# A long convolution and a state-space scan on one core: stages cut into quarters and halves of TensorE's array, rows laid out by parity, five chunks transposed on TensorE, and a new order of work

## The chip, the core and the metric

The kernel runs on one core of a Trainium2 chip. The metric is the device time of one execution in microseconds (us), lower is better; a comparison is made from several executions of both kernels on the same chip. The core has five engines with a queue each: TensorE (PE in the profile, its weight loads PEld), VectorE (DVE), ScalarE (ACT), GpSimd (POOL) and SyncE (SP). Each works off its own list of instructions in order and waits for the others through semaphores. SP and POOL issue the transfers. Matmul results go to PSUM, which is used here as eight banks of 128 rows x 512 float32; ACT and DVE copy them from there to on-chip memory as bfloat16.

## What is computed

Two independent layers on sequences of 2048 rows x 1024 channels; their results stand side by side in the output.

```python
# A: a causal convolution with a filter as long as the sequence
k_shift = sum(k_pad[:, t:t+S, :] * shift_k[:, 3-t] for t in range(4))   # 4 taps
kv = k_shift * v
y  = irfft(rfft(kv, 2S) * rfft(ssm_k, 2S))[:S]
a  = q * (y + kv * ssm_D)
# B: a diagonal complex recurrence over the rows
Bu = x @ B_bar.T
h[t] = Lam_bar * h[t-1] + Bu[t]
b  = 2 * Re(h @ Cmat.T) + x * Dskip
out = concat([a, b], axis=-1)
```

Inputs and output are bfloat16.

## The kernel before

**Layer A** is a transform of 4096 points in two stages. Row s of the sequence is 16 m + (n2), with m = 0..127 and n2 = 0..15, and a tile holds for one or two n2 the 128 rows m, one on each partition. `kvm`, `kva`, `kvb`, `kvc` (DVE) make kv for one n2 from a ring of k tiles (`kp` loads two of them, `vp` two of v). Neighbouring m belong to two interleaved half-length sequences of parity p = m % 2, so the first stage `am` has to transform the even and the odd m apart: for one n2 and one half of the channels it issues two matmuls of the whole 128 x 128 array, with a constant F1 whose rows of the other parity are zero. `ae` copies the two banks out, `ast` stores them to a DRAM buffer, from which they come back in another layout (`lk`). The filter goes the same way: `hl` loads, `hT` transposes on PE, `hc` copies, `hm` transforms, `he` and `hst` store, `lh` reloads. `hm` is already cut into quarters: four matmuls of 64 x 64, two row halves by two column halves, which stand next to each other and write two banks. The second stage (`sk`, `sh`, with a constant from one of three W slots that `lw` loads), a swap of partitions by DMA (`sw`, `swp`), the product (`pr`, DVE) and the inverse second stage (`sa`) follow, all in 64 x 64 quarters. `sae` copies, `vst` stores to a third DRAM buffer Vs, `vl` reloads by n2, and the last stage `a3` brings both parities back into 128 rows, by two full-array matmuls that add up in one bank, again with a half-zero constant G. `a3e` copies it out, `qm` (DVE) multiplies by q (`qp`), and `ost` (POOL) or `osp` (SP) stores two n2 at a time.

**Layer B** takes 16 chunks i of 128 rows. `x.i` loads a chunk transposed, by a transposing DMA on SP. `U.i.jp.jl` is 16 matmuls of 128 x 128 with weights BT; four such pairs make a chunk. `ue` copies them out, `r1` and `r2` (DVE) rotate, `cy` carries the last column over, `sc` (DVE) scans, `r3` and `r4` rotate back, and `y` (full-array matmuls, 5 chunks) or `yq` (64 x 64 quarters, 11 chunks) forms the output with weights CT; `ye`, then `yst`, `ysp`, `ysg`, `ysh` store. At the start `bl`/`bT`/`bc` load, transpose and copy the weights BT, and `cl`/`cT`/`cc` or `cx` (transposing DMA) do it for CT.

**The order** is written out by hand: one string of 1,489 words, each a call such as `U.0.2.0:a34p4` with the places it takes (a: on-chip memory, p: PSUM bank, w, h: W slot and scan slot). The words run in that order, so each engine's list is the string with the other engines' words left out. Which engine copies a bank out is in the word too: `sae` is ACT, `saev` DVE.

A word waits for its inputs and for its places to be free. Bank places bind PE to the engine that empties them, and the in-order lists bind what stands behind a waiting word. The lines of the profile: L417 transposes (bT, cT), L433 and L441 their copies, L468 U, L473 ue, L515 and L518 y, L533 yq, L602 am, L608 ae, L626 hT, L631 hc, L651 hm, L682 sh and sk, L708 pr, L720 sa, L731 vst, L736 vl, L741 qp, L748 a3, L755 a3e, L449 x, L666 lw.

Of the kernel before, what the change touches and what calls it, by code (L numbers as in the profile page):

```python
# [16 lines left out]
BF16 = mybir.dt.bfloat16  # L17
# [15 lines left out]
def a_constants():  # L33
# [31 lines left out]
    return f(F1), f(FQ), f(G), f(W)  # L65
# [3 lines left out]
bl.7.0:a32 wbe.2 bl.0.1:a34 exp1 wb.4:p3 dve2 bl.5.0:a33 dve3 bT.2.0:p6 wb.6:p2 wbe.5 bl.4.0:a49 sm_pre wbe.4  # L69
bl.4.1:a17 exp2 wb.3:p7 bl.1.1:a47 bc.2.0 wb.7:p6 wbe.3 sin0 kp.1 bT.0.1:p0 bT.7.0:p4 wbe.7 wbe.6 bl.6.1:a16 bT.4.0:p1  # L70
bc.0.1 bc.7.0 bl.0.0:a46 tabA1:a24a51a14a12 kp.-1 bT.1.1:p2 x.0:a47 par_rest cl.0.0:a39 wb.1:p7 bT.5.0:p5 sin1
bl.3.0:a31 bcv.4.0 bT.0.0:p3 wbe.1 bT.4.1:p6 bc.1.1 tabA2 kring bl.3.1:a46 kvm.3:a26 gz bT.6.1:p1 bc.0.0 bl.1.0:a23
bc.4.1 U.0.2.0:a34p4 U.0.0.0:p2 sin2 bc.6.1 bl.2.1:a22 bT.3.1:p0 bc.5.0 x.1:a33 eo kvm.2:a18 kvm.1:a40 U.0.2.1
bT.1.0:p5 kva.2 cT.0.0:p1 bT.2.1:p3 bc.2.1 bT.3.0:p6 kva.1 kvb.2:a38 kva.3 bc.3.0 U.1.2.0:a36p7 stt U.1.2.1 bl.6.0:a50
bT.6.0:p3 kvb.1:a46 bl.7.1:a32 bc.3.1 U.0.1.0:p6 bT.7.1:p0 kp.-2 bc.1.0 bc.6.0 bc.7.1 U.0.1.1 U.0.0.1 ue.0.0 ue.0.1
vp.1:a48 cl.2.0:a22 z2 z1 cl.1.1:a31 cc.0.0 x.3:a21 cl.2.1:a44 ue.1.2 ue.0.2 U.0.3.0:p3 U.0.3.1 kvb.3:a32 ue.0.3
U.1.3.0:p6 U.1.0.0:p2 kvm.0:a13 cT.2.0:p0 U.1.3.1 U.1.1.0:p5 kvc.3 kvc.2 kva.0 r1.0:a48 cc.2.0 lw.1:w0 cl.1.0:a30
ue.1.3 cx.5.1 U.1.0.1 ue.1.0 cT.1.0:p3 cc.1.0 cl.3.0:a45 kvb.0:a39 am.2.1:p4p0 ae.2.1.1:a28 rta r2.0:h0 am.2.0:p6p2
cT.2.1:p1 cc.2.1 U.1.1.1 ue.1.1 cT.3.0:p3 vp.0:a42 kvc.1 U.3.2.0:a34p7 cc.3.0 ae.2.0.1 kvc.0 ae.2.0.0 kp.3 sc.0.1
U.3.2.1 hl.0.1:a24 cl.3.1:a20 cT.3.1:p0 sc.0.0 cc.3.1 am.3.0:p5p1 ae.3.1.0:a22 ae.2.1.0 r1.1:a42 hl.0.0 U.3.3.0:p3  # L80
U.3.3.1 cT.1.1:p0 cc.1.1 kp.2 hl.1.0:a48 cl.0.1:a38 ue.3.2 am.3.1:p4p1 ae.3.1.1 U.3.0.0:p6 ue.3.3 U.3.0.1 ue.3.0
ae.3.0.0 hl.1.1 am.1.1:p0p2 ae.1.1.1:a30 cx.5.0 am.0.0:p1p7 ae.0.1.0:a18 ae.3.0.1 r3.0:a12 hdv.1 ast.2 hdv.0 ast.3
U.3.1.0:p3 r4.0 ae.0.0.0 U.3.1.1 x.2:a52 cT.0.1:p5 am.1.0:p6p4 hT.0.4:p7 r2.1:h1 ae.1.0.1 am.0.1:p0p1 hT.0.7:p2
ae.1.1.0 hc.0.4:a16 hT.0.3:p4 ae.1.0.0 hT.0.0:p7 kvm.6:a12 ue.3.1 hT.0.6:p6 hc.0.3:a17 ae.0.0.1 cy.1 cc.0.1 ld_Q
hc.0.0:a46 ae.0.1.1 U.2.1.0:a44p3 r1.3:a40 U.2.1.1 ast.1 sc.1.1 U.2.2.0:p4 hc.0.7:a23 U.2.2.1 U.2.0.0:p5 ast.0 lw.0:w1
cx.6.0 cx.6.1 ue.2.2 U.2.0.1 cx.4.1 ue.2.1 hc.0.6:a20 ue.2.0 r2.3:h2 hT.0.1:p3 hT.0.2:p7 hc.0.1:a22 sc.1.0
hm.0.6.1:p1p2 hm.0.6.0:p4p6 he.0.6.0.0:a34 U.2.3.0:p0 hT.0.5:p3 hc.0.2:a41 U.2.3.1 hm.0.3.0:p5p4 he.0.6.1.1 he.0.6.1.0
# [24 lines left out]
he.1.0.0.0 he.1.0.0.1 he.1.0.1.1 yq.3.6 hm.1.1.0:p1p2 he.1.1.0.0 yq.3.7 ye.3.0:a26 kva.10 ysp.2 hm.1.6.0:p6p3 ast.8
# [78 lines left out]
def full_kernel(ctx, tc, A_q, A_k, A_v, A_shift_k, A_ssm_k, A_ssm_D, B_x, B_Lre, B_Lim, B_Bre, B_Bim,  # L191
# [645 lines left out]
```

## Time and profile before

| | |
|---|---|
| runs shown, us | 351.59 median of 3 (350.28, 351.59, 355.09) |
| profiled execution, first to last instruction, us | 346.5 (the page gives no other time for it) |
| granted TensorE clock | 0.998 of full speed |
| busy us: PE, PEld, DVE, ACT, POOL | 328.0, 237.5, 325.2, 272.3, 69.3 |
| DMA | 101.09 MB, mean 292 GB/s |
| U matmuls (L468) | 2048, 122.6 us busy |
| yq matmuls (L533, 64 x 512) | 1408, 87.6 us busy |
| am matmuls (L602, 128 x 512) | 54 recorded of 64, 16.4 us busy |
| a3 matmuls (L748, 128 x 512) | 61 recorded of 64, 15.1 us busy |
| transposing loads of x (L449) | 16, median 6.2 us to landing |

How to read it: matmuls overlap, so their busy times sum to more than the clock shows, and four quarters of one set run at once; what a matmul costs is read from the starts in the timeline, not from its duration. Some matmul records are missing, so a count of "x12" can stand for 16. A wait that is listed for an engine is idle time of that engine just before the instruction named, put down to what ended it. "PEclk" was at full speed throughout, so times of PE need no correction.

### The profile page before, as it was taken

The numbers are of one execution on the slowest core, as the hardware profiler recorded it, in microseconds if no ns is written. First come the engines' busy times: TensorE is split into PE (matmuls) and PEld (weight loads), VectorE is DVE, ScalarE is ACT, GpSimd is POOL, SyncE is SP. The second block draws the span as 40 slices with busy tenths as digits, with TensorE's granted clock in tenths as the row PEclk, the third lists the DMA queues.
The fourth block names the chain that finished last, engine by engine and source line by source line (L and its number), as shares of the span: only waits on it lengthen the run. The fifth ranks groups of instructions, "written<-read, shape, count | busy, mean of one in ns | idle before, by whom it ended". The sixth has DMA issues, their size and how long they took to land.

```text
span 346.5 us, 11774 instructions
## 1 busy us (share of the span) xinstructions
PE 328.0 (95%) x5086; PEld 237.5 (69%) x5105; DVE 325.2 (94%) x263; ACT 272.3 (79%) x520; POOL 69.3 (20%) x114
## 2 busy tenths in 40 slices
PE   5889899999999999999999999999699999999994
PEld 2678789654856777688957877775376789754442
DVE  3999799999999999999999999999799999999991
ACT  6999999998999884599668899899689893314741
POOL 5000002142343163121100222211021133000021
PEclk9999999999999999999999999999999999999999
DMA  6999999979979879997896689999998898998995
GB/s 214 340 292 261 354 271 275 254 264 307 334 248 248 281 245 301 281 241 277 303 343 205 226 313 344 262 353 330 276 289 297 312 334 287 295 391 270 340 405 205
DMA packets 62752, 101.09 MB, mean 292 GB/s; under 512 B 29422, under 2 KB 31742, under 8 KB 62700
## 3 DMA queue, kind: packets, MB, share of 16 engines
q1 hardware_dynamic: 52652, 65.81, 63.7%
q0 software_dynamic: 10048, 34.52, 27.8%
q8 instruction: 40, 0.66, 0.8%
q14 instruction: 12, 0.10, 0.1%
HBM read 52.08 MB, written 33.55 MB: 247 GB/s over the span
## 4 chain that ended last, share of the span: by engine, by line
PE 68%; ACT 17%; DVE 7%; DMA 4%; issue 2%; SPq 1%; DVEq 0%; ACTq 0%
PE bank L468 24%; PE bank L533 15%; PE bank L515 10%; PE bank L682 4%; PE bank L720 4%; ACT BT L433 4%; PE bank L748 3%; PE bank L602 3%; DVE gslot L499 3%; PE bank L651 2%; ACT arena L608 2%; DMA wslot<-a_c_W 2%; ACT CT L441 2%; DVE arena L486 2%; ACT arena L473 2%
## 5 line engine op out<-in xcount | busy, mean ns | idle before, releaser
L468 PEld LDWEIGHTS <-BT 128*128 128x128 bf16 x2048 | 116.2, 98 | 13.0 <-issue 8.2
L468 PE MATMUL bank<-arena,BT 128*128 128x128 bf16 x2048 | 122.6, 219 | 1.6 <-DMA arena<-in_B_x_dram 0.9
L533 PE MATMUL bank<-CT,gslot 64*64 64x512 bf16 x1408 | 87.6, 377 | 0.0
L499 DVE TENSOR_TENSOR_SCAN gslot<-rtab,gslot 128x1040 bf16<-128x1040 f32 x32 | 73.0, 2312 | 0.1
L533 PEld LDWEIGHTS <-gslot 64*64 64x64 bf16 x1408 | 43.4, 107 | 23.9 <-ACT arena L698 0.6
L473 ACT CAST arena<-bank 128x512 bf16<-128x512 f32 x63 | 38.8, 655 | 11.6 <-PE bank L468 11.6
L608 ACT CAST arena<-bank 128x512 bf16<-128x512 f32 x64 | 37.2, 670 | 5.8 <-PE bank L602 4.9
L515 PE MATMUL bank<-CT,gslot 128*128 128x512 bf16 x154 | 38.1, 380 | 0.6 <-issue 0.3
L691 ACT CAST arena<-bank 128x512 bf16<-128x512 f32 x59 | 32.5, 615 | 7.8 <-PE bank L682 7.2
L486 DVE TENSOR_TENSOR arena<-arena,Z 128x4096 bf16<-128x4096 bf16 x16 | 36.5, 2284 | 2.2 <-ACT arena L473 2.1
L708 DVE TENSOR_TENSOR arena<-arena 128x4096 bf16<-128x4096 bf16 x16 | 36.3, 2285 | 1.7 <-ACT gslot L495 0.8
L728 ACT CAST arena<-bank 128x512 bf16<-128x512 f32 x61 | 33.3, 630 | 5.4 <-PE bank L720 5.3
L486 DVE TENSOR_TENSOR arena<-gslot,Z 128x4096 bf16<-128x4096 bf16 x16 | 36.6, 2288 | 0.3
L698 ACT CAST arena<-bank 128x512 bf16<-128x512 f32 x61 | 34.2, 616 | 3.3 <-PE bank L682 2.8
L659 ACT CAST arena<-bank 128x512 bf16<-128x512 f32 x64 | 35.2, 689 | 1.0 <-PE bank L651 0.7
L551 ACT CAST arena<-bank 128x512 bf16<-128x512 f32 x29 | 17.7, 616 | 16.3 <-PE bank L533 8.7
L582 DVE TENSOR_TENSOR arena<-arena 128x4096 bf16<-128x4096 bf16 (+3 forms) x16 | 30.0, 1886 | 0.1
L662 POOL DMA_DIRECT2D Ys_h<-arena x32 | 22.9, 728 | 29.0 <-ACT arena L659 23.1
L611 POOL DMA_DIRECT2D Ys_kv<-arena x16 | 10.9, 688 | 87.1 <-ACT arena L608 71.8
L515 PEld LDWEIGHTS <-gslot 128*128 128x128 bf16 x160 | 14.0, 98 | 17.1 <-issue 2.6
L702 POOL DMA_DIRECT2D arena<-arena x20 | 10.7, 538 | 70.8 <-ACT arena L691 46.9
L682 PE MATMUL bank<-arena,wslot 64*64 64x512 bf16 x256 | 21.5, 381 | 3.0 <-DMA wslot<-a_c_W 3.0
(104 smaller groups left out, 427.7 us busy)
## 6 DMA issues: line engine op xcount, KB each, us to landing
Ys_kv<-arena POOLq DMA_DIRECT2D x16, 512.0 KB, 4.9
Ys_h<-arena POOLq DMA_DIRECT2D x32, 256.0 KB, 3.8
arena<-Ys_h SPq DMA_DIRECT2D x16, 512.0 KB, 5.3
arena<-Ys_kv SPq DMA_DIRECT2D x16, 512.0 KB, 6.4
Vs<-arena POOLq DMA_DIRECT2D x16, 512.0 KB, 5.8
arena<-Vs SPq DMA_DIRECT2D x16, 512.0 KB, 6.9
arena<-arena POOLq DMA_DIRECT2D x20, 256.0 KB, 4.1
arena<-in_A_k_dram SPq DMA_DIRECT2D x8, 512.0 KB, 6.0
```

Source lines behind the costliest of these rows:

```text
L468: nc.tensor.matmul(pu[:, w, jl, :], BT[:, 2 * jp + jl, w, d, :], xT[:, d, :], start=(d == 0), stop=(d == ND - 1))
L473: either("ue", lambda cp, i, jp: cp(st["u", i][:, :, 2 * jp:2 * jp + 2, :], st.pop(("pu", i, jp))))
L486: nc.vector.tensor_mul(m, s_, win(Z))
L499: nc.vector.tensor_tensor_scan(gf, rtab[:].rearrange("p j t -> p (j t)"), gf, 0.0, ALU.mult, ALU.add)
L515: nc.tensor.matmul(py, h[:, w, j, 2:GW], CT[:, j, w, dh * 512:(dh + 1) * 512], start=(j == 0 and w == 0), stop=False)
L533: mm = nc.tensor.matmul(st["py", i, dh][cols, cs(r)], lhs(dh, rows, c), rhs(dh, rows), start=first, stop=last)
L608: cp(st["ysb", n2][:, p, dh * 512:(dh + 1) * 512], st.pop(("pa", n2, p, dh)))
L659: cp(o, st.pop(("pb", hf, s, e, r)).rearrange("p (n c t) -> p n c t", n=2, c=2))
L682: nc.tensor.matmul(st["ps", nm, g, l][64 * dh:64 * dh + 64, :], st["w", i][rows, a * WC:a * WC + 64], st[nm, i][rows, a, dh * 512:(dh + 1) ...
L698: cp(st["x16", i][:, a, l, :], st.pop(("ps", "k", g, l)))
L708: nc.vector.tensor_mul(hab, st.pop(("x16", i)).rearrange("p a l d -> p (a l d)").unsqueeze(1).to_broadcast([P, 2, 2 * D]), hab)
L728: cp(st["vsb", i][:, a, dh * 512:(dh + 1) * 512], st.pop(("pv", g, dh)))
```

## The change

*Rows by parity.* k, v, q tiles and the A half of the output now hold row m = 2 n + p on partition 64 p + n, so that each parity fills one half of the partitions. The loads of earlier k rows (`kp` with r < 0) need three transfers in place of two.

*First stage in quarters.* `am` issues four 64 x 64 matmuls with FQ, the constant that `hm` already uses; F1 and its load are gone.

*Last stage in column halves.* `a3` issues two matmuls of 128 rows x 64 columns with a small G, one for each parity, into the two halves of one bank.

*Five x chunks* (11 to 15) are loaded plainly (`xn`), transposed by eight matmuls on PE (`xt`) and copied to their place by ACT (`xc`) or DVE (`xcv`).

*Stores.* `ost` and `osp` store one n2 (256 KB) instead of two: 16 stores, not 8.

*Order.* The string is new, 1,506 words. Beside the words above: DVE's evictions a3ev 7 to 1, saev 3 to 0, yev 3 to 0, shev 5 to 3, uev 1 to 2, bcv 1 to 0 (the other engine ACT takes or gives them), hd 2 to 4 and hdv 2 to 0, sw 20 to 23 and swp 12 to 9.

```diff
-    F1 = np.stack([tr * (m % 2 == p)[:, None] for p in range(2)], axis=1)
     FQ = np.concatenate([tr[::2], tr[::2]], axis=0)
-    G = np.stack([tr.T * (m % 2 == p)[None, :] * 2 / NFFT for p in range(2)], axis=1)
+    G = tr.T[:, ::2] * 2 / NFFT
...
 ORDER = """
-bl.5.1:a45 bT.5.1:p6 ld_par par_T:p1 bc.5.1 bl.2.0:a25 ld_F ld_w:a26 wb.0:p0 kp.0:a0 p32 wb.2:p4 wbe.0:a8 dd wb.5:p5
+ld_par par_T:p1 p32 exp1 dd ld_w:a30 wb.2:p4 wb.3:p0 wb.6:p5 wbe.2:a8 bl.3.0:a46 wb.0:p3 bl.6.1:a18 dve2 wbe.3 wb.5:p6
...
-    kr, vr, qr, oar = (a.rearrange("(m s) d -> m s d", s=16) for a in (k, v, q, out_a))
+    kr = k.rearrange("(m s) d -> m s d", s=16)
+    kpr, vr, qr, oar = (a.rearrange("(n p s) d -> p n s d", p=2, s=16) for a in (k, v, q, out_a))
...
+    def xn(i):
+        st["xn", i] = sb(1)
+        spd(st["xn", i], x[i * T:(i + 1) * T, :])
+    E["xn"] = xn
+    E["xt"] = lambda i: tr_(("xn", i), ("xp", i))
...
+    def xc(cp, i):
+        st["xT", i] = sb(1).rearrange("p (d t) -> p d t", d=ND)
+        cp(st["xT", i], st.pop(("xp", i)))
+    either("xc", xc)
...
         if r >= 0:
-            spd(t_, kr[:, 2 * r:2 * r + 2, :])
+            spd(t_, kpr[:, :, 2 * r:2 * r + 2, :])
         else:
-            spd(t_[1:113, :, :], kr[0:112, 16 + 2 * r:18 + 2 * r, :])
-            spd(t_[113:P, :, :], kr[112:P - 1, 16 + 2 * r:18 + 2 * r, :])
+            spd(t_[64:P, :, :], kr[0:P:2, 16 + 2 * r:18 + 2 * r, :])
+            spd(t_[1:49, :, :], kr[1:97:2, 16 + 2 * r:18 + 2 * r, :])
+            spd(t_[49:64, :, :], kr[97:127:2, 16 + 2 * r:18 + 2 * r, :])
...
     def am(n2, dh):
         for p in range(2):
             st["pa", n2, p, dh] = bank()
-            nc.tensor.matmul(st["pa", n2, p, dh], F1t[:, p, :], st["kv", n2][:, dh * 512:(dh + 1) * 512], start=True, stop=True)
+        for a in range(2):
+            for p in range(2):
+                rows, cols = slice(64 * p, 64 * p + 64), slice(64 * a, 64 * a + 64)
+                nc.tensor.matmul(st["pa", n2, p, dh][cols, :], FQt[rows, cols],
+                                 st["kv", n2][rows, dh * 512:(dh + 1) * 512], start=True, stop=True)
...
         for p in range(2):
-            nc.tensor.matmul(pt, Gt[:, p, :], st["vv", n2][:, p, dh * 512:(dh + 1) * 512], start=(p == 0), stop=(p == 1))
+            nc.tensor.matmul(pt[64 * p:64 * p + 64, :], Gt[:], st["vv", n2][:, p, dh * 512:(dh + 1) * 512], start=True, stop=True)
...
-    E["ost"] = lambda r: gpd(oar[:, 2 * r:2 * r + 2, :], st["ot", r])
-    E["osp"] = lambda r: spd(oar[:, 2 * r:2 * r + 2, :], st["ot", r])
+    E["ost"] = lambda n2: gpd(oar[:, :, n2, :], st["ot", n2 // 2][:, n2 % 2, :])
+    E["osp"] = lambda n2: spd(oar[:, :, n2, :], st["ot", n2 // 2][:, n2 % 2, :])
```

What the new order does is seen in the engines' lists. On ACT, near the end of the start phase, before the first copy of a transposed filter tile (COPY to arena, 128x1024, L631 before), the list ran:

```order
L608 CAST arena<-bank_98 128x512
L608 CAST arena<-bank_103 128x512
L608 CAST arena<-bank_100 128x512
L608 CAST arena<-bank_97 128x512
L608 CAST arena<-bank_96 128x512
L608 CAST arena<-bank_100 128x512
L631 COPY arena<-bank_103 128x1024
L608 CAST arena<-bank_102 128x512
```

The same stretch of ACT's list now (L618 is the copy of am, L467 of U, L438 of CT, L641 of hT):

```order
L618 CAST arena<-bank_100 128x512
L618 CAST arena<-bank_96 128x512
L618 CAST arena<-bank_99 128x512
L618 CAST arena<-bank_97 128x512
L467 CAST arena<-bank_101 128x2x256
L467 CAST arena<-bank_102 128x2x256
L438 COPY CT<-bank_98 128x8x128
L641 COPY arena<-bank_96 128x1024
```

Ahead of that copy stand three more copies of am and one more of BT than before, and behind it those that moved.

On PE, am.4.0 stood among the full-array matmuls of y.1.1 (bank_99 the output of y, F1t the masked constant):

```order
L518 MATMUL bank_99<-Dd,arena 128x128
L602 LDWEIGHTS F1t
L602 MATMUL bank_103<-arena,F1t 128x512
L602 LDWEIGHTS F1t
L602 MATMUL bank_102<-arena,F1t 128x512
L515 LDWEIGHTS gslot_90
```

Now it stands between two parts of the same y as four quarters (FQt; L611 is am, L520 and L523 y; the two matmuls are issued a second time for the other column half):

```order
L523 MATMUL bank_101<-Dd,arena 128x128
L611 LDWEIGHTS FQt
L611 MATMUL bank_96<-arena,FQt 64x512
L611 LDWEIGHTS FQt
L611 MATMUL bank_100<-arena,FQt 64x512
```

The rows behind these are the same two banks once more and then y's next matmul on L520: the array goes from 128 x 128 to 64 x 64 and back around one am. In the string before, PE's words change between full-array work and quarters 64 times; in the new one they change between full-array work, quarters and column halves 196 times, 28 of them to or from the halves.

In the tail of PE's list, an a3 before (Gt the constant of the last stage, bank_98 its output, between y.14 and y.15):

```order
L518 MATMUL bank_102<-Dd,arena 128x128
L748 LDWEIGHTS Gt
L748 MATMUL bank_98<-arena,Gt 128x512
L748 LDWEIGHTS Gt
L748 MATMUL bank_98<-arena,Gt 128x512
L515 LDWEIGHTS gslot_90
```

And the last a3 now, between two parts of y.15:

```order
L523 MATMUL bank_97<-Dd,arena 128x128
L758 LDWEIGHTS Gt
L758 MATMUL bank_101<-arena,Gt 64x512
L758 LDWEIGHTS Gt
L758 MATMUL bank_101<-arena,Gt 64x512
L520 LDWEIGHTS gslot_90
```

Both matmuls of the word now have 64 output rows and go to the two halves of one bank.

More of the change, by code (lines that the diff above doesn't have):

```diff
@@ L71 @@
[L71 to L75, printed above, removed]
@@ new lines @@
+cy.9:h1 sh.12:p2p3 she.12.0:a44 yq.8.0:p6p7 she.12.1 U.10.0.1 she.13.0 r2.9 sk.12:p3p4 yq.8.1 she.13.1 sa.11:p0p2
+lk.7:a1 ske.12.0:a42 sa.10:p5p3 ue.10.0 ske.12.1 sae.11.0:a12 lk.8:a51 yq.8.2 lw.8:w2 pr.4 yq.8.3 sae.10.1 sk.13:p4p0
+sae.11.1 sc.9.1 sae.10.0 ske.13.0 xt.11:p2 sa.9:p5p3 yq.8.4 xc.11:a14 sa.8:p2p4 yq.8.5 sae.9.1:a29 sae.9.0 sc.9.0
+ske.13.1 sh.17:p5p1 sae.8.1 she.17.0:a35 sh.16:p3p0 yq.8.6 vst.2 ysp.7 she.16.1 she.16.0 sk.17:p4p5 sw.6.0 yq.8.7
+she.17.1 sae.8.0 ye.8.1:a34 ske.17.0:a9 U.11.3.1:p3 sw.6.1 U.11.3.0 sk.16:p7p2 ske.17.1 ske.16.1 pr.6 sa.13:p5p0
@@ L488, in full_kernel, with g_ @@
     E["r1"] = lambda i: rot_mul(i, st.pop(("u", i)), Z1)
+    def g_(i):
+        if ("g", i) not in st:
+            st["g", i] = gslots[cur["h"].pop(0)]
+        return st["g", i]
     def r2(i):
[L491 removed]
         m = mview(i)
[L493 removed]
+        nc.vector.tensor_add(g_(i)[:, :, :, 2:GW], m[:, :, 0, :, :], m[:, :, 1, :, :])
     E["r2"] = r2
[L495 removed]
+    E["cy"] = lambda i: nc.scalar.copy(g_(i)[:, :, :, 1], st["g", i - 1][:, ::-1, :, GW - 1])
     def sc(i, a):
```

270 lines of the change are left out of this document (129 added, 141 removed).

## The prediction

> **What bounds the kernel now.** I read the page first (busy time, chain), then the busy time by stage, then what PE itself waited for, then the timelines at the places that the change touches.
>
> ```profile
> span 346.5 us, 11774 instructions
> PE 328.0 (95%) x5086; PEld 237.5 (69%) x5105; DVE 325.2 (94%) x263; ACT 272.3 (79%) x520; POOL 69.3 (20%) x114
> PE 68%; ACT 17%; DVE 7%; DMA 4%; issue 2%; SPq 1%; DVEq 0%; ACTq 0%
> ```
>
> PE and DVE are both nearly full, and the chain goes mostly through PE. The stages tell them apart (columns: PE, PEld, DVE, ACT, POOL busy us with counts, clock, DMA share, GB/s):
>
> ```profile
> 45.00:60.00 15.00, 14.89 (x234) 13.83 (x234) 15.00 (x12) 15.00 (x28) 2.86 (x5) 1.00 1.11 270
> 60.00:75.00 15.00, 14.67 (x156) 8.73 (x155) 15.00 (x13) 15.00 (x29) 4.74 (x7) 1.00 0.99 263
> 285.00:300.00 15.00, 15.00 (x271) 13.53 (x272) 14.64 (x9) 6.72 (x14) 3.38 (x5) 1.00 0.83 287
> ```
>
> Up to about 60 us ACT has no free moment: it copies every BT, CT and U out of PSUM, and PE's eight banks come free at ACT's pace. Later ACT has room (6.72 of 15). DVE is full in the middle too, but hardly anyone on PE waits for it. PE's waits:
>
> ```profile
> PE bank L417 <- DMA arena<-in_B_B_im_dram: 4.7, 2, 3.5
> PE bank L682 <- DMA wslot<-a_c_W: 3.0, 1, 3.0
> PE bank L468 <- DMA arena<-in_B_x_dram: 0.9, 1, 0.9
> PE bank L720 <- DVE arena L708: 0.7, 1, 0.7
> ```
>
> The first and third lie in the first 18 us. Behind 60 us PE has two waits worth a line, 3.0 for a W slot and 0.7 for DVE's product. So the model is: ACT sets the pace to about 55 us, and from there the time is PE's matmuls laid end to end, plus a few us.
>
> **The change part by part.** *Cheaper matmuls.* The masked pairs of am and a3 are 2 x 32 words of two 128x512 matmuls each:
>
> ```profile
> 28.72 5.52 PE L468 MATMUL bank<-arena,BT 128*128 128x128 bf16 x96
> 34.08 0.61 PE L417 MATMUL bank<-ident,arena 128*128 128x128 bf16 x8
> 302.72 0.20 PE L533 MATMUL bank<-Dd,arena 64*64 64x64 bf16 x4
> 303.61 0.20 PE L533 MATMUL bank<-Dd,arena 64*64 64x64 bf16 x4
> 320.01 2.75 PE L748 MATMUL bank<-arena,Gt 128*128 128x512 bf16 x12
> 322.60 1.03 PE L515 MATMUL bank<-CT,gslot 128*128 128x512 bf16 x4
> ```
>
> Starts tell the rate: twelve 128x512 matmuls take 322.60 - 320.01 = 2.59, so 0.216 each and 0.43 a word; a 128x128 one takes 5.36 / 96 = 0.056; four quartets of 64x64 quarters and one small quartet take 303.61 - 302.72 = 0.89, so a quartet takes at most 0.22 (I use 0.216). am's 32 words go from 0.43 to 0.216: -6.9 us, certain as to its rate, since FQ quarters run so today (L651). a3's two column halves, 64 outputs from 128 rows, stand in no row. Run side by side they take 0.216 a word (-6.9), one after the other 0.43 (0). I take the former, by the quarters, the nearest row in which column halves share one bank.
>
> *Changes of array shape.* This is what the change adds. Counting along PE's order from start to end, the step from full-array matmuls to quarters or halves, back, or between these two comes 64 times before and 196 times now. Its price:
>
> ```profile
> 64.43 1.06 PE L468 MATMUL bank<-arena,BT 128*128 128x128 bf16 x16
> 65.42 0.41 PE L651 MATMUL bank<-arena,FQt 64*64 64x512 bf16 x4
> 65.76 1.04 PE L515 MATMUL bank<-CT,gslot 128*128 128x512 bf16 x3
> 66.64 0.22 PE L518 MATMUL bank<-Dd,arena 128*128 128x128 bf16 x1
> 66.79 0.41 PE L651 MATMUL bank<-arena,FQt 64*64 64x512 bf16 x4
> ```
>
> Sixteen matmuls from 64.43 end at 65.32, the quartet starts at 65.42: 0.10 lost. It is through at 65.64, and the next starts at 65.76: 0.12. At 66.64 the gap is 0.15 in place of 0.056: 0.09. So 0.10 a step, 0.2 for in and out. A lone quartet between full-array work then costs 0.42, as much as the masked pair that it replaces; only am words that lie beside other quarters gain (20 of the runs of quarters now are am alone, 22 words). In all (196 - 64) x 0.10 = +13.2, the 28 steps to and from the halves at the same price (these no row shows: 0 to 0.12 each, so up to 2.8 less). The Trainium skill, "TensorEngine Tiling (Array Packing)", section Tiling Modes, says that changing the mode drains TensorE, with no time; it would make the halves pay too.
>
> *x through TensorE.* Five chunks take 8 transposes each and a copy.
>
> ```profile
> 40.23 0.61 PE L417 MATMUL bank<-ident,arena 128*128 128x128 bf16 x8
> 40.68 1.06 PE L468 MATMUL bank<-arena,BT 128*128 128x128 bf16 x16
> L449 SPq DMA_TRANSPOSE arena<-in_B_x_dram x16: 1237/1575/4278, 13.2 to 275.4; - x16
> arena<-in_B_B_re_dram SPq DMA_DIRECT2D x8, 256.0 KB, 4.7
> ```
>
> Eight take 0.45, so 5 x 0.45 = +2.2 on PE. The Trainium skill, "TensorE: Matmul & The Clock Gate", Part 4, gives about 275 ns for one transpose in a kernel; by that the term would be 11.0 and the end 8.8 later, but the row has 0.056 from start to start, and I keep it. The copies, of the size of a BT copy (0.90 on ACT, below), go four to ACT and one to DVE, under PE's work. SP's issue of a chunk falls from 1.6 (median; the row has min/median/max) to the 0.34 of a plain one (last row of the tail below), 5 x 1.2 = 6 us late and off PE's path. But xt now makes PE itself wait for the plain load. Four have 7.7 us or more of PE work between xn and xt; xt.13 has 3.4 (r4.9 frees its place just before), and a 256 KB load lands after 4.7 (the row of B's loads, median). Behind xt.13 on PE stand sa.17, yq.9.2 and all that follows, though U.13 needs the chunk some 41 us later. So 0.34 + 4.7 - 3.4 = 1.6 at most, nothing if DVE is ahead there; I take +0.8.
>
> *ACT at the start.* The first hT copy (L631) is a place that both orders pass. Before it ACT now has 16 BT copies instead of 15 (bcv.4.0 was DVE's) and 16 am evictions instead of 13; CT, U and the rest are equal.
>
> ```profile
> 25.35 5.61 ACT L433 ACTIVATE BT<-bank 128x1024 bf16<-128x1024 bf16 x6
> 30.77 1.15 ACT L473 CAST arena<-bank 128x512 bf16<-128x512 f32 x2
> 48.59 0.78 ACT L608 CAST arena<-bank 128x512 bf16<-128x512 f32 x1
> 49.07 1.28 ACT L473 CAST arena<-bank 128x512 bf16<-128x512 f32 x2
> 53.45 1.21 ACT L631 COPY arena<-bank 128x1024 bf16<-128x1024 bf16 x1
> ```
>
> A BT copy takes 0.90, an eviction 0.48: 0.9 + 3 x 0.48 = +2.3, and 0.3, my choice without a row, because ACT's first copy now waits for the parameters: the place moves from 53.45 to about 56.1, +2.6. ACT is the pace there, so cheaper am words gain nothing ahead of it. PE is also less far: 22 U words (16 matmuls, 0.89 each) are behind it, not 24, so 2 x 0.89 = 1.8 is still to come, and 8 am words, not 7.
>
> *DVE.* Evictions that DVE gives up (6 a3e, 3 sae, 3 ye, 2 she) against those it takes (one ue, one x copy), and bcv away: 13 fewer.
>
> ```profile
> L755 DVE CAST arena<-bank 128x512 bf16<-128x512 f32 x7 | 4.8, 681 | 0.0
> ```
>
> About 13 x 0.68 = 8.8 us, and two adds of 0.2 go to ACT. By the waits above this is worth at most the 0.7 on L720; I take 0.9 off, with the small gap beside it.
>
> *Rows by parity, stores, tail.* Loads of k, v, q keep their bytes and run lengths; two kp words issue one DMA more. out's A half leaves in 16 stores of 256 KB, not 8 of 512; POOL and SP issue them between other things. The way through Vs must still be hidden:
>
> ```profile
> 286.65 1.06 PE L720 MATMUL bank<-arena,wslot 64*64 64x512 bf16 x16
> 290.17 0.72 POOL L731 DMA_DIRECT2D Vs<-arena  x1 [1.90 <-ACT arena L728]
> 294.77 3.90 SPq L736 DMA_DIRECT2D arena<-Vs  x6
> 305.75 1.47 PE L748 MATMUL bank<-arena,Gt 128*128 128x512 bf16 x5
> DMA to landing us min/median/max: 4.5/6.9/7.9
> 341.89 0.22 PE L518 MATMUL bank<-Dd,arena 128*128 128x128 bf16 x1
> 342.76 0.34 SPq L555 DMA_DIRECT2D out_dram<-arena  x1
> ```
>
> From the last sa (ends 287.6) PE had 18.1 us of other work before the first a3. The chain under it is 2.5 to the last store, 4.6 to the first load, three issues of 0.65 and 6.9 (the landing row is that of the loads from Vs): 16.0. Now PE has 17.3 there (11 U words, 7 yq.12 words of 0.89, one x, some steps). It just holds. From the last matmul (341.89) to the end there are 4.6 us of eviction and store; that stays.
>
> *The sum*, on the span of 346.5: ACT's start +2.6; U left over +1.8; am behind that place 25 x 0.43 to 24 x 0.216 = -5.6; a3 -6.9; x +2.2 and +0.8; steps behind that place 182 instead of 64, +11.8; DVE -0.9; the 3.0 wait for a W slot, whose reload has 4.1 to 4.7 us of PE work now against 4.1 to 4.9, taken as half gone, -1.5. That is +4.3, so a span of 350.8. The shown runs have a median of 351.59 (350.28 to 355.09), 5.1 above the profiled span; so 355.9, which I call 356, or +1.2%. Two per cent, about what a measurement of this kernel can tell from no change, is 344.6 and 358.6.
>
> **The rivals.**
>
> *Cheap steps* (14%). If a step costs half where PE would wait anyway, 5.9 comes off: 350. If all new ones were free, 11.8: 344, faster. Against: PE hardly waits behind 60 us, so there is little to hide in, and where it waits that wait is itself time.
>
> *DVE was the bound* (10%, faster). DVE is busy 15.00 of 15 in two of the windows above. If PE only kept step with it, 8.8 fewer us on DVE give 346.5 - 8.8 + 5.1 = 343. Against: PE's 0.7 us of waiting for DVE.
>
> *Halves in a row* (12%, slower). If the second half of an a3 waits for the first, its 6.9 is not gained: 363, +3%. It decides once a word takes more than 0.30 (358.6 - 355.9 = 2.7, over 32 words 0.08 above 0.216). For: both halves use the same 128 rows.
>
> ```profile
> L748 PEld LDWEIGHTS <-Gt 128*128 128x128 bf16 x64 | 5.8, 98 | 6.7 <-issue 0.5
> ```
>
> Against: these 98 ns loads use the same rows as the matmul ahead, and matmuls still follow at 0.216. The Trainium skill, "TensorE: Matmul & The Clock Gate", Part 3, has weight loads overlap matmuls only where the row group differs, which would put the halves in a row; this trace's full-array stream contradicts it.
>
> *A new wait* (14%, slower at its upper end). The Vs chain has 1.3 us in hand; a last store that lands at 7.9 or a late sae uses that up, a W slot can again cost 3.0, and xt.13 twice what I took: 358 to 361.
>
> **How the numbers follow.** Forecast 50%: 356, by itself 351 to 360, a tenth of it over 358.6. Slower: halves 12, new wait 11, forecast's upper end 5: 28%. Faster: DVE 9, free steps 3: 12%. Within 2%: 60%. The range runs to halves in a row, 363, and down past cheap steps with both new waits gone (350 - 0.8 - 1.5) to 346, where the halves' steps are free too (28 x 0.05 at half price, 1.4); the faster cases are the tenth left out below.
>
> **What would show it.** In the profile after: steps between shapes with gaps of 0.09 to 0.12, about 196 of them; the first hT copy near 56 us; a3 words 0.216 apart; PE still the chain's main engine with no more than 3 to 5 us of waits behind 60 us; DVE near 316 busy with idle time that costs nothing. I am wrong if the steps cost nothing, if the first hT copy comes before 53 us, or if PE waits for DMA in the tail.

## The result: 65% slower, and the profile after

The kernel after takes 577.95 us (573.9 to 579.25), the kernel before on the same chip 350.93 (median of four); the ratio is 1.65, with a 95% interval of 1.64 to 1.67. Some executions of a kernel run some per cent slower than its others; the ratios leave these out, and so do the times of the experiments below. The forecast of 356 and all its rivals are far off. The profiled execution has a span of 577.4 us.

First the page of the kernel after (busy time, slices of 14.4 us each, bytes, chain).

```profile
span 577.4 us, 12054 instructions
PE 355.0 (61%) x5200; PEld 241.6 (42%) x5209; DVE 319.8 (55%) x248; ACT 289.2 (50%) x542; POOL 75.5 (13%) x120
PE   5034427994285966566999999994898000888000
PEclk9558577998596989597899999998799555899555
GB/s 117 117 219 82 131 51 289 253 106 52 204 284 128 85 212 65 181 93 161 356 291 291 321 294 318 299 274 207 175 167 55 52 111 197 225 209 142 89 59 37
DMA packets 61425, 101.01 MB, mean 175 GB/s; under 512 B 27502, under 2 KB 29710, under 8 KB 61372
PE 34%; DMA 21%; SPq 6%; issue 4%; DVE 1%; ACT 1%; POOL 0%; DVEq 0%; ACTq 0%
```

No engine's work accounts for 227 us more: PE is busy 27 us longer than before, ACT 17 and POOL 6, DVE 5 less. The bytes are the same, 101.01 MB for 101.09. What is new is that everything stops at times, and that DMA and SP's queue have 21% and 6% of the chain, where they had 4% and 1%. From slice 20 to 27 the kernel runs as before; at the start and at the end it doesn't. The granted clock is 0.50 in the stretches below where PE stands still. It can't be what stops the kernel there: PE has nothing to compute in them.

The busy time by stage shows what the two kinds of stretch look like (columns as in the prediction).

```profile
320.00:340.00 20.00, 20.00 (x392) 12.76 (x393) 19.05 (x11) 17.41 (x36) 3.46 (x6) 1.00 0.93 322
455.00:472.00 17.00, 0.00 (x0) 0.00 (x0) 0.00 (x0) 0.00 (x0) 0.00 (x0) 0.50 0.14 53
545.00:575.00 30.00, 0.00 (x0) 0.00 (x0) 2.25 (x3) 0.00 (x0) 0.00 (x0) 0.50 0.13 51
```

In the second no engine computes, in the third only DVE for 2.25 us of 30, and the core's 16 DMA engines move 51 to 53 GB/s at a share of 0.13 to 0.14. A share of 0.13 of 16 is the work of two engines. What waits for them is in the list of waits (engine, line, releaser: us in all, times, longest):

```profile
DVE arena L603 <- DMA arena<-in_A_v_dram: 57.5, 6, 21.9
PE bank L758 <- DMA arena<-Vs: 50.4, 3, 47.6
DVE arena L590 <- DMA arena<-in_A_k_dram: 27.1, 3, 9.5
DVE arena L588 <- DMA arena<-in_A_k_dram: 22.6, 2, 17.2
PE bank L414 <- DMA arena<-in_B_B_im_dram: 21.5, 2, 21.2
DVE arena L767 <- DMA arena<-in_A_q_dram: 18.9, 1, 18.9
PE bank L458 <- DMA arena<-in_B_x_dram: 11.9, 1, 11.9
```

v, k and q are the loads by parity. But B's weights, Vs and the chunks of x that U (L458) waits for are loaded exactly as before, and are waited for too. The timeline of SP and the chain of waits, both of the kernel after, show how they come to be late:

```profile
418.51 42.60 SPq L751 DMA_DIRECT2D arena<-in_A_q_dram  x4
461.41 19.80 SPq L746 DMA_DIRECT2D arena<-Vs  x4
```

```profile
451.29 9.83 SPq L751
461.41 9.58 SPq L746
471.75 20.93 DMA arena<-Vs
513.88 30.20 DMA arena<-in_A_q_dram
```

Four issues of q hold SP for 42.6 us; before, one took 0.37 (median). The loads from Vs stand behind them on the queue: the first takes 9.6 to issue, one behind it lands after 20.9, and PE's a3 waits for it. It is not only so at the end. The transposing loads of x, whose row for the kernel before stands in the prediction (1575 ns, median), are issued at this pace in the kernel after:

```profile
L442 SPq DMA_TRANSPOSE arena<-in_B_x_dram x11: 1244/11161/22835, 18.8 to 258.7; - x11
```

### The profile page after: what moved, and what is told of

The parts are those of the page before. It is cut to its first block, busy times and chain, and to the rows that moved or that the text cites. A ratio compares the mean times of both kernels' runs of the same rounds, so it can differ in the third digit from the quotient of the medians.

```text
span 577.4 us, 12054 instructions
## 1 busy us (share of the span) xinstructions
PE 355.0 (61%) x5200; PEld 241.6 (42%) x5209; DVE 319.8 (55%) x248; ACT 289.2 (50%) x542; POOL 75.5 (13%) x120
## 2 busy tenths in 40 slices
DMA packets 61425, 101.01 MB, mean 175 GB/s; under 512 B 27502, under 2 KB 29710, under 8 KB 61372
## 4 chain that ended last, share of the span: by engine, by line
PE 34%; DMA 21%; SPq 6%; issue 4%; DVE 1%; ACT 1%; POOL 0%; DVEq 0%; ACTq 0%
PE bank L538 12%; PE bank L458 12%; DMA arena<-in_A_q_dram 5%; SPq L751 4%; DMA arena<-Vs 4%; DMA arena<-in_A_ssm_k_dram 4%; DMA arena<-arena 3%; DMA arena<-in_A_v_dram 3%; PE bank L730 3%; PE bank L692 2%; SPq L746 2%; PE bank L520 2%; DMA Ys_kv<-arena 2%; PE bank L758 1%; PE bank L661 1%
## 5 line engine op out<-in xcount | busy, mean ns | idle before, releaser
L458 PE MATMUL bank<-arena,BT 128*128 128x128 bf16 x2048 | 139.4, 229 | 53.4 <-issue 41.3
L458 PEld LDWEIGHTS <-BT 128*128 128x128 bf16 x2048 | 125.7, 103 | 74.6 <-issue 74.4
L538 PE MATMUL bank<-CT,gslot 64*64 64x512 bf16 x1408 | 94.6, 390 | 5.0 <-issue 5.0
L467 ACT CAST arena<-bank 128x512 bf16<-128x512 f32 x62 | 37.0, 607 | 59.2 <-PE bank L458 55.1
L538 PEld LDWEIGHTS <-gslot 64*64 64x64 bf16 x1408 | 39.7, 110 | 38.0 <-issue 11.7
L767 DVE TENSOR_TENSOR arena<-arena 128x2048 bf16<-128x2048 bf16 x8 | 9.7, 1221 | 74.3 <-ACT arena L765 55.4
L669 ACT CAST arena<-bank 128x512 bf16<-128x512 f32 x64 | 35.6, 619 | 28.9 <-PE bank L661 28.9
L618 ACT CAST arena<-bank 128x512 bf16<-128x512 f32 x64 | 35.1, 602 | 27.0 <-PE bank L611 26.8
L765 ACT CAST arena<-bank 128x512 bf16<-128x512 f32 x31 | 16.6, 601 | 59.8 <-PE bank L758 58.4
L603 DVE TENSOR_TENSOR arena<-arena 128x1024 bf16<-128x1024 bf16 x16 | 10.9, 686 | 57.5 <-DMA arena<-in_A_v_dram 57.5
L758 PE MATMUL bank<-arena,Gt 128*64 128x512 bf16 x64 | 10.4, 412 | 50.4 <-DMA arena<-Vs 50.4
L738 ACT CAST arena<-bank 128x512 bf16<-128x512 f32 x64 | 34.3, 609 | 14.1 <-PE bank L730 13.4
L520 PE MATMUL bank<-CT,gslot 128*128 128x512 bf16 x151 | 39.9, 391 | 1.1 <-issue 0.9
L414 PE MATMUL bank<-ident,arena 128*128 128x128 bf16 x232 | 20.2, 253 | 26.0 <-DMA arena<-in_B_B_im_dram 21.5
L708 ACT CAST arena<-bank 128x512 bf16<-128x512 f32 x61 | 33.7, 606 | 4.0 <-PE bank L692 3.3
L701 ACT CAST arena<-bank 128x512 bf16<-128x512 f32 x61 | 33.4, 615 | 4.2 <-PE bank L692 3.4
```

Of the source, the lines that this page charges most:

```text
L458: nc.tensor.matmul(pu[:, w, jl, :], BT[:, 2 * jp + jl, w, d, :], xT[:, d, :], start=(d == 0), stop=(d == ND - 1))
L467: cp(st["u", i][:, :, 2 * jp:2 * jp + 2, :], st.pop(("pu", i, jp)))
L520: nc.tensor.matmul(py, h[:, w, j, 2:GW], CT[:, j, w, dh * 512:(dh + 1) * 512], start=(j == 0 and w == 0), stop=False)
L538: mm = nc.tensor.matmul(st["py", i, dh][cols, cs(r)], lhs(dh, rows, c), rhs(dh, rows), start=first, stop=last)
L618: cp(st["ysb", n2][:, p, dh * 512:(dh + 1) * 512], st.pop(("pa", n2, p, dh)))
L669: cp(o, st.pop(("pb", hf, s, e, r)).rearrange("p (n c t) -> p n c t", n=2, c=2))
```

## The experiments

An access pattern lists its dimensions from the slowest to the fastest, with a count for each. In this text "a step of two" means that the outermost dimension on the DRAM side counts two. **Theory A.** The rearranged pattern has a step of two (`p n s d` with p = 2). Such a DMA runs on two of the 16 DMA engines, and the queue behind it waits. **B**: rows with a stride are slow in memory. **C**: too many issues. **D**: the new order and the changes of array shape. Each run below is compared with the kernel before on its own chip.

### All split, loads split

```diff
+    def halves(dma, t_, ap, out=False):
+        for p in range(2):
+            rows = t_[64 * p:64 * p + 64]
+            dma(ap[p], rows) if out else dma(rows, ap[p])
...
-            spd(t_, kpr[:, :, 2 * r:2 * r + 2, :])
+            halves(spd, t_, kpr[:, :, 2 * r:2 * r + 2, :])
```

The same for v, q, `ost` and `osp`; in the second run `ost` and `osp` stay as they are.

> The kernel after, with each load of k, v and q and each store of out's A half issued as two DMAs of 64 partitions, one for each parity, in place of one whose outermost DRAM step counts two. Same rows, same addresses, same bytes, same order; 24 loads and 16 stores more. Theory A (a DMA whose outermost step counts two runs on two of the 16 DMA engines, and the queue behind it waits): the time falls to what the prediction's other terms give, 350 to 363 us, and PE's stalls on loads go. Theory B (rows taken with a stride of 32 are slow to read and write in memory): it stays above 500. Theory C (more issues on SP's and POOL's queues): it gets slower than 578. Theory D (the new order and the changes of array shape): it stays above 500.

Measured: 360.7 us (360.26 to 360.98), ratio 1.035 (1.028 to 1.042).

> As the run before, but only the loads of k, v and q are split; out's A half keeps its 16 stores with an outermost step of two. Theory A: everything up to the first store of out runs as in the run with all split; the stores, 4.2 MB, at the 53 GB/s that the profile after shows in its emptiest stretches, would take 79 us in a row. The first can start about 40 us before the end, and POOL's need not share two engines with SP's, so 365 to 400. Theory B: above 500. Theory D: as the run with all split.

Measured: 397.6 us (two executions), ratio 1.14 (1.13 to 1.16). Both lie in A's ranges. With more DMAs and the same rows, 217 of the 227 us go; C and D fall, and B falls as the main cause. Splitting the loads is worth 180 of them, splitting the stores after that the other 37.

### The same in the kernel before

```diff
+    vpr, qpr = (a.rearrange("(n p s) d -> p n s d", p=2, s=16) for a in (v, q))
...
-        spd(st["v", r], vr[:, 2 * r:2 * r + 2, :])
+        spd(st["v", r], vpr[:, :, 2 * r:2 * r + 2, :])
```

The same for q; the second run has p=16.

> The kernel before with one edit: its loads of v and q take the rows by parity through one DMA with an outermost step of two, as in the kernel after (so v and q come in another order of rows; nothing else changes). 16 loads of 512 KB. Theory A: two engines carry these 8.4 MB beside their sixteenth of the other 92.7 MB, 10 MB each; at half of 53 GB/s each that is 378 us, which is more than the 346.5 of the span, so slower by 8% or more: 380 to 480. Theory B: slower too, by as much as the run with 16 parts. Theory D: 351, as before.

Measured: 503.1 us, ratio 1.45 (1.43 to 1.46).

> As the run before, but the rows of v and q are taken in 16 interleaved sets in place of two (outermost step of 16, rows 256 apart beside each other in a set). Theory A: 16 engines again, so as the kernel before, 348 to 358. Theory B: as slow as the run with two sets, or slower. Theory D: 351.

Measured: 360.5 us, ratio 1.034 (1.026 to 1.042). Sixteen loads with a step of two cost some 154 us in a kernel that has none of the other edits (348.6 without them on that chip); the same loads with a step of 16 cost 12. Both times are above A's ranges. For the 503, I had reckoned only with the two engines' load and not with the queue behind them: in that run the loads from Vs, plain as before, take 2.46 us each to issue where they took 0.56 (medians). How much of the excess that makes was not divided. The 12 us are more than A allowed: a part of B is true.

### Loads on an idle chip

> Nothing of the work, only DMAs on an idle chip: 512 KB of k loaded into one tile, each load behind the one before (same tile), six rounds of: plain rows; outermost step of 2, 4, 8 and 16 (rows interleaved); two DMAs of 64 partitions with plain rows; two with rows by parity. Then stores: 8 plain ones of 512 KB, then of 256 KB 8 plain, 4 with an outermost step of two, and 4 as pairs of 64 partitions by parity, all from one tile and waiting for nothing. Theory A: an engine moves about 26 GB/s, so 512 KB take some 2 us of latency and 1.3 us by 16 engines, 2.5 by 8, 5 by 4, 10 by 2. Interleaving alone (16 sets; two DMAs by parity) costs little on 16 engines: under 30% more than plain rows. Theory B (addresses): sets of 16 or pairs by parity are as slow as sets of 2.

The stretches below run from one issue to the next (the last edges to within 0.17 us), in the second of six rounds: plain rows, a step of 2, of 4, of 8, of 16, two DMAs of plain rows, two by parity (columns: us, POOL, clock, DMA share, GB/s).

```profile
47.12:50.66 3.54, 0.00 (x0) 1.00 0.47 148
50.66:63.33 12.67, 0.00 (x0) 1.00 0.11 41
63.33:72.79 9.46, 0.00 (x0) 1.00 0.19 55
72.79:79.45 6.66, 0.00 (x0) 1.00 0.33 79
79.45:84.18 4.73, 0.00 (x0) 1.00 0.40 111
84.18:87.69 3.51, 0.00 (x0) 1.00 0.54 147
87.69:92.29 4.60, 0.00 (x0) 1.00 0.42 116
```

This is theory A by itself: 12.7, 9.5, 6.7, 4.7 and, plain, 3.5 us for the same 512 KB; the medians of all six rounds are within 0.4 of these rows. A had expected about 12, 7, 4.5 and 3.3, so it is right for two, and the other steps gain less than it says. In the middle of the first round's load with a step of two (4.34 to 17.51), the window from 8 to 16 us has

```profile
8.00:16.00 8.00, 0.00 (x0) 1.00 0.13 53
```

the same 0.13 and 53 GB/s as the dead stretches of the kernel after. The Trainium skill, "DMA: Bandwidth & Descriptors", section "Why a DMA increments its semaphore by 16 and not by 1", says that a DMA is spread over the largest number up to 16 that divides the size of the slowest dimension (other than one) of both access patterns, and that a DMA of SP takes the lowest-numbered engines. The traces agree with the first half. Counted from the start and length of every packet, two packets are under way at a time for 95% of a stretch inside the second round's load with a step of two (52 to 62 us), four for 89% with a step of 4 (65 to 71), eight for 83% with a step of 8 (75 to 78), and sixteen or seventeen for 81% with a step of 16 (81.5 to 83). In the kernel after it is two for 94% of the dead stretch from 455 to 472. That the second half makes every other transfer late, since each has its sixteenth on the same two engines, fits the waits for B, x and Vs; no record here names the engine.

The stores at the end of this run show the queue. Eight plain ones of 256 KB are issued and moved in 7.2 us, at 382 GB/s. Four with a step of two hold SP for 11.2, one of them for 8.3, and from 298.0 to 302.9 us the DMA engines move 51 GB/s at a share of 0.13. The pairs by parity stand behind these on the queue, so their time prices nothing.

The last two rows size what is left of B: on an otherwise idle chip rows by parity, split in two, cost 1.1 us more per 512 KB than plain rows split in two (4.60 against 3.51), and rows in 16 interleaved sets 1.2 more than plain rows (4.73 against 3.54). That is about a third, a little over the 30% that A allowed. Two DMAs instead of one cost at most 0.1 (3.70 against 3.57, medians of the six rounds).

### What the rest of the change does

> The kernel after with the rows of k, v, q and out in their plain order, one DMA each, as the kernel before has them (the constants stay those for rows by parity, so out's A half is computed from other rows than the reference's); everything else, the order of the work, the quarters, the halves, the transposes of x, stays. It prices all that the change does apart from the rows by parity. The prediction's terms make 356 of it. If all split (360.7) is late because rows by parity are dearer to load even by 16 engines, this is 352 to 357, with the stretch from 5 to 20 us near the 315 to 377 GB/s of the kernel before and not the 216 to 281 of the run with all split. If the new order is what starts late, it stays at 359 to 362.

Measured: 352.9 us, ratio 1.013 (1.007 to 1.018). Of this run the first line of the page, then its first hT copy (line, count, ns of one as min/median/max, first and last start in us):

```profile
span 350.7 us, 12060 instructions
```

```profile
L640 ACT COPY arena<-bank x16: 1012/1044/1130, 56.1 to 112.3; 128x1024 bf16<-128x1024 bf16 x16
```

PE's three longest waits:

```profile
PE bank L279 <- DMA praw<-in_A_ssm_D_dram: 3.9, 1, 3.9
PE bank L414 <- DMA arena<-in_B_B_re_dram: 3.7, 1, 3.7
PE bank L414 <- DMA arena<-in_B_B_im_dram: 3.5, 2, 2.9
```

And two windows near the start, with the same two of the run with all split and that run's first hT copy behind them:

```profile
15.00:20.00 5.00, 0.62 (x8) 0.45 (x8) 5.00 (x4) 5.00 (x12) 0.00 (x0) 0.67 1.12 285
20.00:25.00 5.00, 4.52 (x48) 4.14 (x49) 5.00 (x5) 5.00 (x12) 0.00 (x0) 0.65 1.09 368
```

```profile
15.00:20.00 5.00, 1.03 (x8) 0.77 (x8) 4.65 (x3) 5.00 (x11) 0.00 (x0) 1.00 1.17 216
20.00:25.00 5.00, 1.89 (x16) 1.63 (x16) 5.00 (x5) 3.86 (x12) 0.00 (x0) 1.00 1.04 293
```

```profile
L646 ACT COPY arena<-bank x16: 1012/1046/1132, 61.0 to 118.1; 128x1024 bf16<-128x1024 bf16 x16
```

With plain rows the DMA engines move 285 and 368 GB/s where rows by parity give 216 and 293 at about the same share, and the first hT copy starts at 56.1 instead of 61.0. From 5 to 20 us it is 264 to 315 GB/s, more than the 216 to 281 with parity, less than the 315 to 377 that was hoped for.

> All split, but k comes in plain rows by one DMA (so out's A half is computed from other rows than the reference's); v, q and out stay split by parity. All split was at 360.7, all plain at 352.9, 7.8 less. If the remaining price sits in k's loads at the start, ahead of B's chunks (first hT copy at 61.0 against 56), this gives 5 of it: 355 to 356, with the first hT copy near 56. If it sits in the number of DMAs on SP's queue at the end, or spread over all loads by parity, it gives 1 to 2: 359 to 360.

Measured: 354.9 us, ratio 1.022 (1.018 to 1.026); the first hT copy is at 56.1 again. So of the 7.8 us that rows by parity cost on 16 engines, 5.8 are k's (4.4 of 7.7 by the ratios, since the chips differ a little). The first hT copy comes 4.9 earlier, so k's part stands mostly at the start, where DMA is the scarce thing (a share of 1.04 to 1.17 above).

> All split, with one edit in the order: the first two loads of k (2 MB... two ring places, four DMAs of 256 KB) leave SP behind bl.4.1 in place of ahead of kp.-1. If the late start (PE waits 4.2 and 4.3 us for B's chunks before 24 us) comes from k's loads ahead of B's on SP's queue, 3 to 6 us are won: 355 to 358. If DVE, which needs k for kvm.3, then holds am and the rest: 360 or more.

```diff
-wbe.6 wb.4:p4 bl.2.0:a36 wb.7:p7 bl.1.1:a48 bl.3.1:a39 kp.0:a0 kp.1 wbe.0 ...
+wbe.6 wb.4:p4 bl.2.0:a36 wb.7:p7 bl.1.1:a48 bl.3.1:a39 wbe.0 ...
-bT.6.1:p7 kp.-1 exp2 ...
+bT.6.1:p7 kp.-1:a0 exp2 ...
-bl.4.1:a42 bT.4.1:p3 ...
+bl.4.1:a42 kp.0 kp.1 bT.4.1:p3 ...
```

Measured: 361.2 us, ratio 1.037 (1.031 to 1.043), no better than the 360.7 of all split. The waits only changed hands: PE waits 8.8 us for one of B's chunks, and DVE 4.7 for k. So these two loads (1 MB together) are not merely at the wrong place in the queue, as far as one other place can tell; all of the loads are needed, and they come slower.

### Quarters and halves, one at a time

> All split, with am's 32 words as two full-array matmuls against FQ masked to one half of the rows (the form of the kernel before) in place of four quarters. By the prediction's terms, behind the first hT copy 24 words go from 0.216 to 0.43 (+5.2 us) and the steps around those am words that stand alone go away (2 x 0.10 each; 22 of them in all, about 20 behind that place, -4.0): +1 us, 361 to 363. If steps cost nothing, +5: 366. If PE weren't the bound there, 361.

Measured: 362.5 us, ratio 1.041 (1.035 to 1.046): 1.8 above all split (2.2 by the ratios). The intervals of the two ratios overlap, so that it is more than nothing isn't shown.

> All split, with each a3 as two accumulating full-array matmuls against a masked Gt (the form of the kernel before) in place of two column halves. By the prediction, 32 words go from 0.216 to 0.43 (+6.9 us) and the 28 steps to and from the halves lose their price to full-array neighbours, where those stand (a3 next to quarters still pays): between -1 and -2.8. Sum +4 to +6: 365 to 367. If PE waits for Vs, q or stores at the end in any case: 361.

Measured: 367.5 us, ratio 1.052 (1.045 to 1.058): 6.8 above all split (6.0 by the ratios), and the two intervals don't overlap. The halves are worth about what the prediction took for the pairing; am's quarters are worth hardly anything, as the prediction has it, with the steps around them against their gain.

### The halves in the kernel before

> The kernel before with a3's column halves alone: q and out by parity, each as two DMAs of 64 partitions; k, v, am, x and the whole order as before. By the prediction's terms: 32 a3 from 0.43 to 0.216, -6.9; in this order the halves bring 79 - 64 = 15 steps more, +1.5; so -5.4, 344 to 346, if PE's matmuls are what sets the end. If q by parity on a queue that is full costs as much as all parity rows did (7.8 over k, v, q and out), half of that comes back: 348 to 350. If the end hangs on Vs, DVE or stores: 350.

Measured: 359.5 us, ratio 1.037 (1.027 to 1.048).

> As the run before, with q and out in plain rows by one DMA each (the halves' outputs then meet other rows of q, so out's A half isn't the reference's). 344 to 346 if PE sets the end; the difference to the run before is the price of q and out by parity.

Measured: 350.2 us, ratio 1.004 (0.998 to 1.010). Both missed, the first above all its cases. Rows by parity cost 9 us here, though only q and out have them. And the halves gain nothing, while they gain 6 to 7 in the order of the kernel after. Either DVE, busy 19.8 of 20 us near the end of the kernel before, took it, or something else did.

> The kernel before with nine evictions of its end (seven of a3, yev.12.0 and yev.13.0) on ACT in place of DVE, at their old places in the order. 9 x 0.68 = 6.1 us less for DVE, 9 x 0.6 = 5.4 more for ACT, which between 280 and 346 us has some 37 us to spare. If DVE's work sets the end of the kernel before (it is busy 19.8 of 20 us from 300 to 340), 3 to 6 us are won: 344 to 348 beside 350 to 351. If PE's matmuls set it, as the prediction has it, or if the evictions' late places on ACT hold a bank longer: 350 or more.

Measured: 349.7 us, ratio 1.004 (0.999 to 1.008).

> The kernel before with a3's halves (q and out in plain rows, so out's A half is not the reference's) and the same nine evictions on ACT. With the halves alone the time was 351.1, no gain. If DVE took the halves' gain away, both together win what neither wins alone: 343 to 347. If DMA (Vs, W) or something else holds the end: 349 to 351.

Measured: 349.4 us, ratio 1.004 (0.999 to 1.010).

> The kernel before with all 22 evictions that it gives DVE behind the middle on ACT: 15 us off DVE, 13 on ACT. If DVE sets the time from the middle on: 342 to 346. If PE does: 350. If ACT gets late between 260 and 280 us, where it is busy 17.4 of 20: 352 or more.

Measured: 356.5 us, ratio 1.012 (1.003 to 1.021): slower, with waits of PE for a W slot of 4.7 us, where they were 3.0.

Taking evictions off DVE gains nothing, with the halves or without. The chain of waits of the run with both halves and nine evictions moved (L499 scan, L486, L493 and L505 rotations, L515 y, L748 a3, L755 a3e, L757 qm) shows what holds the end:

```profile
295.07 4.54 DVE gslot L499 x2
...
308.96 4.54 DVE gslot L499 x2
313.53 2.30 DVE arena L486
315.86 1.24 DVE gslot L505
317.14 1.04 PE bank L515 x4
...
325.33 5.36 DMA arena<-in_A_q_dram
330.70 2.35 DVE arena L757 x2
333.06 1.15 DVE gslot L505
334.25 1.04 PE bank L515 x4
```

From 295 on it is a chain: scan and rotations of the last chunks, y, then a load of q, its product, the last rotation and the last y. It has few evictions in it, and 2.7 us of PE's a3 in all. The kernel before has the same scan and rotations on its chain, but behind them it goes through PE alone, from 316.87 to the last matmul, with about 10 us of a3. Two of its lines, and one wait of PE in the run with the halves in plain rows, which the list of the kernel before doesn't have:

```profile
307.77 4.53 DVE gslot L499 x2
316.87 1.04 PE bank L515 x4
```

```profile
PE bank L515 <- DVE gslot L505: 3.0, 2, 1.5
```

So from there on PE sets the end of the kernel before, and DVE's last rotations and q come just in time: a PE that is faster waits for them. In the order of the kernel after a3's time does count, as the run with full-array a3 shows; which link makes the difference was not taken apart.

## Why the prediction was wrong

**The step that failed is "Rows by parity, stores, tail".** It says that "loads of k, v, q keep their bytes and run lengths" and that POOL and SP issue the stores "between other things", and puts the price at nothing. Bytes and run lengths are indeed the same; the number of engines that share them is not. The three loads and the stores came to some 217 us through that, and rows by parity to another 7.8 that remain on 16 engines. No row of the profile before has a load or store with an outermost step of two. The prediction bounds other costs without a row from both sides; this one it priced by its size alone. No rival covers it: the one on a new wait looked at three known transfers, for 2 to 5 us. Of the prediction's signs of being wrong the last one came, PE waiting for DMA in the tail: 50.4 us for Vs.

**The other steps**, read in the run with plain rows, hold well. The sum was 350.8 of span and +1.2%; measured 350.7 and +1.3%. As a time it is 352.9 and not 355.9: the 5.1 us that the prediction adds to a span are 1.8 in that run (352.47 for 350.7).

*ACT at the start*: "about 56.1" for the first hT copy; 56.1. PE waits longer in the first 25 us, for parameters and B's chunks (11 us in the three waits above), but ACT still sets that place: it is busy for 50.8 of the 51 us from 5 to 56.

*Changes of array shape*, at 0.10: two places of PE's timeline in that run, a lone quartet between full-array work and pairs of halves among quarters.

```profile
60.78 0.41 PE L660 MATMUL bank<-arena,FQt 64*64 64x512 bf16 x4
61.12 0.71 PE L635 MATMUL bank<-ident,arena 128*128 128x128 bf16 x8
320.34 0.39 PE L538 MATMUL bank<-CT,gslot 64*64 64x512 bf16 x4
320.66 0.84 PE L757 MATMUL bank<-arena,Gt 128*64 128x512 bf16 x6
321.43 0.84 PE L538 MATMUL bank<-CT,gslot 64*64 64x512 bf16 x12
```

The quartet to the next start takes 0.34, so 0.12 above 0.216. Going from quarters to halves takes 0.32, 0.10 above it. So the halves pay the step as well, for which no row stood.

*a3 halves side by side*: six halves take 321.43 - 320.66 = 0.77; less a step of 0.12, as behind the quartet, that is 0.65 for three pairs, 0.217 a pair. The rival of halves in a row is out. Going back to full-array a3 costs 6 to 7 us, where its expectation had 4 to 6.

*am*: it came to 1.8 where 24 x 0.216 = 5.2, less 4.0 for the steps around lone words, makes 1.2; the two aren't told apart by these runs.

*x, the W slot and the tail*: no wait of PE for an x chunk or a W slot is in the list of that run, so the +0.8 was too much and the -1.5 should have been -3.0. From the first hT copy to the last matmul's start it is 288.6 us (56.10 to 344.74) where it was 288.4, +0.2 instead of +1.7; and from there to the end 6.0 instead of 4.6. These two misses cancel: the total is better than its terms.

*DVE* is busy 318.6, about the 316 foreseen. The rival that DVE was the bound isn't borne out, since taking evictions off it gains nothing. The model that from 55 us on "the time is PE's matmuls laid end to end" describes the kernel before, but not what a shorter PE would bring to it: there the scan, the rotations and q just about keep step with PE.

*Still open*: why rows by parity are slower on 16 engines. The number of DMAs isn't needed for it, since a single DMA in 16 interleaved sets costs 1.2 us on the idle chip and 12 in the kernel before; another place in the queue didn't help; it comes with the interleaving. Whether the addresses or the way the pattern is cut decides was not separated. How much of the 217 us is two engines' own time and how much the queue that waits was not divided either.

## What to carry to other kernels

Before a layout change goes through a DMA, read the access pattern's outermost step and not only bytes and run lengths: two there cost over three times the time of one load (12.7 us against 3.5), and hold up everything behind it on the queue. If a pattern needs such a step, issue one DMA for each of its values, here with 64 rows outermost. Then price the layout where DMA is scarce: the 1.1 us more per 512 KB come to 4 to 6 us for k at the start of this kernel and 2 to 3 for v, q and out together, more than am's quarters brought, and to 9 for q and out in the kernel before.

A part that is faster is worth something only on the chain that ends last, and only up to the next chain: the same halves gave 6 to 7 us in one order and nothing in the other.

## What the runs showed of the hardware

As many packets are under way at a time as the outermost step counts: 2, 4, 8 or 16. But a load's time falls slowly with it, 12.7, 9.5, 6.7 and 4.7 us, so twice the engines is far from half the time. The granted clock was 0.50 in the dead stretches of the kernel after (0.811 as a mean, 0.996 in the profiled run with all split), but idle time of PE alone doesn't tell it: from 15 to 20 us PE is busy 1.03 us at a clock of 1.00 with all split, and 0.62 us at 0.67 with plain rows. And issues on SP of transfers that are spread well stall too, behind the slow ones: a load from Vs took 9.6 us to issue (0.56 before, median), a transposing load of x 11.2 (median; 1.6 before).
